# GpSimd reorders, ScalarE casts: swapping two steps of the q/k preparation between engines in an attention-plus-MLP kernel

## The chip, the core and the metric

The kernel runs on one core of one Trainium2 chip, as one program. The metric is the device time of one execution in microseconds. The engines named below are PE (TensorE, matrix multiply), ACT (ScalarE), DVE (VectorE), POOL (GpSimd) and SP (the queue that issues the DMAs). Each engine works through its own queue of instructions strictly in order.

## The reference

Local attention, attention over tokens pooled by four, and an MLP without bias (arrays are float32; B=8, H=8, S=576, D=64):

```python
q_d = q.reshape(B, H, Sd, 4, D).mean(axis=3)      # k_d, v_d alike, Sd = 144
out_d = softmax(scale * q_d @ k_d.T) @ v_d
out_up = np.repeat(out_d, 4, axis=2)
mask = np.abs(pos[:, None] - pos[None, :]) < 4    # a band of 7
out_local = softmax(where(mask, scale * q @ k.T, -1e9)) @ v
x = (out_up + out_local) as [B*S, H*D]            # 4608 x 512
h = x @ w_in                                      # 512 -> 2048
out = (h - tanh(h)) @ w_out                       # 2048 -> 512
```

## The kernel before

The attention is cut into 32 pairs, each two heads of one batch entry; four pairs make one batch entry. Pairs 0 to 7 and pairs 8 to 31 are prepared in two ways. From pair 8 (`EARLY`) on, a pair goes through these steps:

1. SP loads the rows of q and k as float32 into `qkn` (lines 325 to 340), nine tokens of 64 values on each of 64 partitions for each head; v goes to `vst`, and from pair 16 on a second copy of v to `vp`.
2. Two casts (line 490) write bfloat16 copies into `qr`, 128 x 576 each.
3. SP issues a DMA transpose, `qT<-qr` (line 495). Its result holds nine planes of 128 columns.
4. Two copies (line 503) put the planes in token order: `qk<-qT`, one for q and one for k. The input is read with a step of 128 bfloat16 values, the output written without a gap.
5. POOL adds tokens in fours: `half` (line 537) and `qkd` (line 543 or 550).
6. PE multiplies: scores of the band (line 559) and of the pooled part (line 582), in PSUM. ACT takes exponentials (lines 606, 618, 621). The band's mask is either multiplied into the exponentials `E` afterwards (the large one, 128 x 912, at line 610; the small one, 128 x 240, at line 625), or, from pair `FORE` on, the large one is added as a `bias` in PSUM before the exponential (line 601, DVE).
7. PE multiplies with v (lines 634, 640), DVE normalises (653, 655), a DMA transpose `lT<-ln` or PE turns the result, and a join (684, 688, on POOL or DVE) writes `xT`, the input of the MLP.

POOL also casts v (`vw`, line 424) and, from pair 16 on, pools v in two additions (`vp` 386, `vd` 391).

The MLP is `mm1` (line 727, then tanh on ACT at 738 and the subtraction on DVE at 741) and `mm2` (line 763, evacuated at 778 by ACT or DVE into `y`). Its matmuls use four PSUM banks, `ps_hy`.

The order on every engine is fixed when the program is built. The class `Program` holds each step with a cost in ns, its reads and writes and a priority; a list scheduler plays the plan through with these costs and appends the instructions in the order of the planned starts. An attention step of PE goes ahead of MLP matmuls as soon as the plan holds it ready; MLP matmuls fill the rest. A `P.choice` names several engines with a cost each, and the plan takes the one that comes free first. So a cost in the source changes the order of all queues, and where the cost is not the real one, a queue waits at run time.

In the kernel before, the casts of pairs 8 to 15 may run on DVE, ACT or POOL and those from pair 16 (`CASTS`) on POOL; the copies into token order run on ACT, and before pair 12 (`REORD`) also on DVE; `FORE` is 16.

Of the kernel before, what the change touches and what calls it, by code (L numbers as in the profile page):

```python
# [15 lines left out]
class Program:  # L16
# [20 lines left out]
    def op(self, eng, ns, fn, reads=(), writes=(), pri=0):  # L37
        i = len(self.ops)
        deps = set()
        for key in reads:  # L40
            if key in self.last_write:
                deps.add(self.last_write[key])
        for key in writes:
            if key in self.last_write:
                deps.add(self.last_write[key])
            deps.update(self.readers.get(key, ()))
        for key in reads:
            self.readers.setdefault(key, set()).add(i)
        for key in writes:
            self.last_write[key] = i  # L50
            self.readers[key] = set()
        deps.discard(i)
        if eng == "DMA":
            self.moves[i - 1] = i
        self.ops.append((eng, ns, fn, deps, pri))
        self.touch.append(set(reads) | set(writes))
        return i
# [108 lines left out]
def kernel(  # L166
# [83 lines left out]
    P = Program()  # L250
    op = P.op
    V, A, T, GP = nc.vector, nc.scalar, nc.tensor, nc.gpsimd
# [202 lines left out]
    def attention(p):  # L455
# [15 lines left out]
        if LOAD[p] == 'tok':  # L471
            P.choice([(eng, ns, lambda fn=fn: fn(
                out=qr[s].rearrange("p a h d -> p (a h d)"),
                in_=qkn[sn].rearrange("p h c -> p (h c)"))) for eng, ns, fn in CAST_QK],
                     reads=[("qkn", sn, 0), ("qkn", sn, 1)],
                     writes=[("qr", s, 0), ("qr", s, 1)], pri=pri - 12)
            if TIN[p] == 'dma':
                op("SP", 1300, lambda: nc.sync.dma_start_transpose(
                    out=qk[s].rearrange("p i c -> p (i c)").rearrange(
                        "p (t c) -> p t c", c=128),  # L480
                    in_=qr[s].rearrange("p a h d -> p (a h d)")),
                   reads=[("qr", s, 0), ("qr", s, 1)],
                   writes=[("qk", s, 0), ("qk", s, 1), ("qTq", s)], pri=-50)
                op("DMA", 1300, None, reads=[("qTq", s), ("qr", s, 0), ("qr", s, 1)],
                   writes=[("qk", s, 0), ("qk", s, 1)], pri=pri)
        else:
            for hh in range(2):
                dst = qr[s][:, :, hh]
                srt = qkn[sn][:, hh].rearrange("p (a d) -> p a d", d=D)
                P.choice([(eng, ns, lambda dst=dst, srt=srt, fn=fn: fn(out=dst, in_=srt))  # L490
                          for eng, ns, fn in (any3[2:] if p >= CASTS else any3[:1] + any3[2:] if 0 < p < NOACT else any3)],
                         reads=[("qkn", sn, 0), ("qkn", sn, 1)],
                         writes=[("qr", s, hh)], pri=pri - 12)
        if TIN[p] == 'dma' and LOAD[p] == 'row':
            op("SP", 1300, lambda: nc.sync.dma_start_transpose(
                out=qT[s], in_=qr[s].rearrange("p a h d -> p (a h d)")),
               reads=[("qr", s, 0), ("qr", s, 1)],
               writes=[("qT", s), ("qTq", s)], pri=-50)
            op("DMA", T_IN, None, reads=[("qTq", s), ("qr", s, 0), ("qr", s, 1)],
               writes=[("qT", s)], pri=pri)  # L500
            for i in range(2):
                def put(fn, i=i):
                    fn(out=full[:, i].rearrange("p (g a) -> p g a", a=A9),  # L503
                       in_=qT[s][:, :, i::2].rearrange("p a g -> p g a"))
                P.choice([("ACT", 1080, lambda put=put: put(A.copy))] +
                         [("DVE", 750, lambda put=put: put(V.tensor_copy))][:p < REORD],
                         reads=[("qT", s)], writes=[("qk", s, i)], pri=pri)
        elif TIN[p] == 'pe':
            if p in APART:
                parts = [(ps[:, 0].bitcast(BF16), 0, 5, ts, [("qk", s, 0)]),  # L510
                         (po[:, 0].bitcast(BF16), 5, 4, ox, [("qk", s, 1)])]
            else:
                parts = [(ps.rearrange("p b x -> p (b x)").bitcast(BF16), 0, A9, ts,
                          [("qk", s, 0), ("qk", s, 1)])]
            for bank, a0, n, keys, to in parts:
                planes = bank[:, 0:128 * n].rearrange("p (a x) -> p a x", a=n)

                def tr(planes=planes, a0=a0, n=n):
                    for a in range(n):
                        T.transpose(planes[:, a], qr[s][:, a0 + a].rearrange(  # L520
                            "p h d -> p (h d)"), ident)

                def put(fn, planes=planes, a0=a0, n=n):
                    fn(out=full.rearrange("p i (g a) -> p i g a", a=A9)[:, :, :, a0:a0 + n],
                       in_=planes.rearrange("p a (g i) -> p i g a", i=2))
                if a0 == 0:
                    P.fresh.add(len(P.ops))
                op("PE", (56 * n + 40) * cold, tr, reads=[("qr", s, 0), ("qr", s, 1), "ident"],
                   writes=keys, pri=pri)
                P.choice([("ACT", 90 + 98 * n, lambda put=put: put(A.copy)),  # L530
                          ("DVE", 60 + 140 * n, lambda put=put: put(V.tensor_copy))][:2 - (p in PUT_ACT)],
                         reads=keys, writes=to, pri=pri)
# [67 lines left out]
        def add_bias(bank, part):  # L600
            V.tensor_tensor(out=bank, in0=bank, op=ALU.add, in1=bias[:, part].unsqueeze(1)  # L601
                            .to_broadcast([128, 2, part.stop - part.start]))
        if p >= FORE:
            op("DVE", 1025, lambda: add_bias(ps[:, :, 0:456], slice(0, 456)),
# [3 lines left out]
           reads=ts, writes=[("E", s, 0)], pri=pri)  # L608
        if BIASED <= p < FORE:
            P.choice([(eng, ns, lambda fn=fn: fn(  # L610
                out=e1, in0=e1, in1=mask[:, 0:456].unsqueeze(1).to_broadcast([128, 2, 456]),
                op=ALU.mult)) for eng, ns, fn in MASK1[p >= NP]],
# [11 lines left out]
        if not biased:  # L624
            P.choice([(eng, ns, lambda fn=fn: fn(  # L625
                out=e2v, in0=e2v, in1=mask[:, 456:576].unsqueeze(1).to_broadcast([128, 2, 120]),
                op=ALU.mult)) for eng, ns, fn in MASK2[p >= SMALL][p >= FORE:]],
                reads=["mask"], writes=[("E", s, 1)], pri=pri)
# [16 lines left out]
        if p == 2:  # L645
# [13 lines left out]
            op=ALU.mult), reads=ox + [("r", s)], writes=[("ln", s)], pri=pri)  # L659
# [127 lines left out]
    def dense(kb):  # L787
# [6 lines left out]
        for _, second, i in steps:  # L794
# [6 lines left out]
    EARLY, BIASED = 8, 4  # L801
# [12 lines left out]
    INORDER = 6  # L814
    JOIN_V = [p for p in range(8, 32) if p % 4 > 1]
    V_ACT = ()
    FORE = 16
    GATE, BEHIND = range(12, NPAIR), 5
    BYACT = 0
    DIRECT, T_P = 16, 860  # L820
    T_IN, T_OUT = 1550, 1200
    NOACT = 0
    SMALL = 8
    HOLD = 3
    APART = (0, 1)
    LEAD = 0.75
    YOUT = [("ACT", 480, A.copy), ("DVE", 600, V.tensor_copy)]
    CASTS, REORD = 16, 12
    MASK1 = [[("DVE", 760, V.tensor_tensor)]] * 2
    MASK2 = [[("DVE", 300, V.tensor_tensor)], [("DVE", 300, V.tensor_tensor), ("POOL", 630, GP.tensor_tensor)]]  # L830
    T_Q0 = (850, 660), (2170, 1350), (710, 720), (700, 720)
# [6 lines left out]
    any3 = [("DVE", 670, V.tensor_copy), ("ACT", 590, A.copy),  # L838
            ("POOL", 630, GP.tensor_copy)]
# [53 lines left out]
    for p in range(2):  # L893
        prep_v(p)
    work = [attention(p) for p in range(NPAIR)]
    for a in work:
        next(a)
# [61 lines left out]
```

## Time and profile before

| | |
|---|---|
| median of 3 runs | 325.64 us (325.17 to 326.78) |
| the profiled execution | 325.69 us |
| its span, first to last instruction | 323.7 us |
| PE busy | 313.6 us, 97% of the span |
| DVE, ACT busy | 218.9 and 218.7 us, 68% each |
| POOL busy | 190.2 us, 59%, nothing after 250 us |
| granted TensorE clock | 1.00 throughout |

The profiled execution is 2.0 us longer than its span. A row of the profile names the line, the engine, the operation, output<-input by tile, shape and count, then the busy time in us, the mean of one in ns, and the idle time of the engine just ahead of these instructions with what ended it.

### The profile page before, as it was taken

The page shows a single profiled execution, that of the slowest core. Times are in us where ns is not written, and L with a number is a line of the kernel's source. Part 1 is how long each engine was busy: PE and PEld are TensorE (multiplying, and loading weights), DVE is VectorE, ACT ScalarE, POOL GpSimd, SP SyncE. Part 2 cuts the span into 40 slices and gives each one's busy share as a digit, 9 for nine tenths or more (in the row PEclk, how much of TensorE's full clock was granted, in tenths as well). Part 3 has the DMA queues.
Part 4 walks back from the last instruction along what each step waited for, and adds up shares of the span by engine and source line. Part 5 has one row for each costly group of instructions (what it writes and reads, how often), then busy time and mean ns, then how long its engine had stood idle before and what let it go on. Part 6 is the DMA issues. An engine that isn't in the chain of part 4 may idle for free.

```text
span 323.7 us, 7166 instructions
## 1 busy us (share of the span) xinstructions
PE 313.6 (97%) x2648; PEld 174.3 (54%) x2648; DVE 218.9 (68%) x395; ACT 218.7 (68%) x381; POOL 190.2 (59%) x262
## 2 busy tenths in 40 slices
PE   6898999999899999999999999999999999999996
PEld 2464555556654445666654444666654445566544
DVE  7898785678966589787785777777765554554311
ACT  3755886699877976898768877888786334545300
POOL 5658966278656897988887988889844000000000
PEclk9999999999999999999999999999999999999999
DMA  6999999989999899999999999999522211001022
GB/s 198 300 396 334 368 306 343 216 208 233 242 232 202 210 254 225 242 256 251 251 230 284 242 257 212 250 241 284 121 63 61 63 46 52 34 32 34 33 84 79
DMA packets 114515, 64.50 MB, mean 199 GB/s; under 512 B 92848, under 2 KB 97712, under 8 KB 114480
## 3 DMA queue, kind: packets, MB, share of 16 engines
q1 hardware_dynamic: 114480, 64.05, 79.9%
q8 instruction: 20, 0.33, 0.5%
q14 instruction: 15, 0.12, 0.1%
HBM read 42.47 MB, written 9.44 MB: 160 GB/s over the span
## 4 chain that ended last, share of the span: by engine, by line
PE 86%; SPq 5%; DMA 3%; DVE 2%; POOL 1%; issue 1%; ACT 1%; POOLq 0%; ACTq 0%
PE ps_hy L763 38%; PE ps_hy L727 36%; DMA gT<-in_moe_w_in_dram 3%; PE ps_ox L559 3%; PE ps_ox L634 3%; SPq L325 2%; SPq L358 2%; PE ps_ox L640 2%; PE ps_ox L582 1%; PE ps_ox L669 1%; DVE ln L655 1%; PE ps_ox L666 1%; PE ps_ox L520 1%; POOL w_in_sb L417 1%; DVE E L610 1%
## 5 line engine op out<-in xcount | busy, mean ns | idle before, releaser
L727 PE MATMUL ps_hy<-xT,w_in_sb 128*128 128x320 bf16 (+1 forms) x768 | 148.2, 326 | 1.1 <-DVE gT L741 1.1
L763 PE MATMUL ps_hy<-w_out_sb,gT 128*128 128x512 bf16 (+1 forms) x592 | 144.9, 373 | 0.0
L741 DVE TENSOR_TENSOR gT<-ps_hy,u 128x320 bf16<-128x320 f32 (+1 forms) x192 | 103.2, 553 | 61.0 <-ACT u L738 59.0
L738 ACT ACTIVATE u<-ps_hy 128x320 f32<-128x320 f32 (+1 forms) x192 | 92.2, 495 | 49.5 <-PE ps_hy L727 42.6
L727 PEld LDWEIGHTS <-w_in_sb 128*128 128x128 bf16 x768 | 71.8, 98 | 53.9 <-issue 1.5
L763 PEld LDWEIGHTS <-gT 128*128 128x128 bf16 x592 | 56.2, 98 | 53.3
L503 ACT COPY qk<-qT 128x576 bf16<-128x576 bf16 x44 | 52.4, 1208 | 0.0
L537 POOL TENSOR_TENSOR half<-qk 128x576 f32<-128x576 bf16 x29 | 33.3, 1147 | 27.5 <-ACT qk L503 18.9
L490 POOL CAST qr<-qkn 128x576 bf16<-128x576 f32 x51 | 34.4, 690 | 8.1 <-DMA qkn<-in_k_dram 4.6
L655 DVE TENSOR_TENSOR ln<-ps_ox,r 128x896 bf16<-128x896 f32 x32 | 34.9, 1091 | 1.0
L606 ACT ACTIVATE E<-ps_ox 128x912 bf16<-128x912 f32 x28 | 26.1, 932 | 5.0 <-PE ps_ox L559 4.0
L424 POOL CAST vw<-vst 128x640 bf16<-128x640 f32 x32 | 25.0, 781 | 3.8 <-DMA vst<-in_v_dram 3.5
L778 DVE COPY y<-ps_hy 128x512 f32<-128x512 f32 (+1 forms) x20 | 13.3, 663 | 16.7 <-PE ps_hy L763 16.5
L386 POOL TENSOR_TENSOR vp<-vp 72x512 f32<-72x512 f32 x16 | 20.3, 1270 | 1.0 <-DMA vp<-in_v_dram 1.0
L625 POOL TENSOR_TENSOR E<-E,mask 128x240 bf16<-128x240 bf16 x20 | 12.8, 641 | 11.6 <-ACT E L618 10.2
L634 PE MATMUL ps_ox<-vw,E 128*128 128x65 bf16 x320 | 19.6, 194 | 0.0
L634 PEld LDWEIGHTS <-E 128*128 128x128 bf16 x320 | 16.2, 98 | 5.6 <-DVE E L610 0.3
L621 ACT ACTIVATE E<-ps_ox 72x576 bf16<-72x576 f32 (+1 forms) x28 | 18.8, 671 | 0.0
L601 DVE TENSOR_TENSOR ps_ox<-ps_ox,bias 128x912 f32<-128x912 f32 x16 | 17.7, 1109 | 1.5 <-PE ps_ox L559 1.4
L640 PE MATMUL ps_ox<-vd,E 128*128 128x65 bf16 (+1 forms) x256 | 18.3, 193 | 0.1
L559 PEld LDWEIGHTS <-qk 64*128 64x128 bf16 x320 | 9.1, 94 | 15.5 <-issue 11.3
L778 ACT COPY y<-ps_hy 128x512 f32<-128x512 f32 x17 | 10.0, 587 | 7.1 <-PE ps_hy L763 7.1
(83 smaller groups left out, 266.6 us busy)
## 6 DMA issues: line engine op xcount, KB each, us to landing
vst<-in_v_dram SPq DMA_DIRECT2D x64, 160.0 KB, 4.2
qkn<-in_q_dram SPq DMA_DIRECT2D x32, 288.0 KB, 4.3
qkn<-in_k_dram SPq DMA_DIRECT2D x32, 288.0 KB, 4.3
out_dram<-y SPq DMA_DIRECT2D x35, 256.0 KB, 2.5
vp<-in_v_dram SPq DMA_DIRECT2D x16, 288.0 KB
gT<-in_moe_w_in_dram SPq DMA_DIRECT2D x4, 1024.0 KB, 11.0
xT<-in_moe_w_out_dram SPq DMA_DIRECT2D x8, 256.0 KB, 5.1
gT<-in_moe_w_out_dram SPq DMA_DIRECT2D x2, 1024.0 KB, 8.5
```

The costliest lines, as they stand in the source:

```text
L424: P.choice([(eng, ns, lambda fn=fn: fn(out=vw[w][:, 2 * jj:2 * jj + 2, :, 0:64], in_=vst[s])) for eng, ns, fn in CAST_V[p >= NEARLY]], rea ...
L490: P.choice([(eng, ns, lambda dst=dst, srt=srt, fn=fn: fn(out=dst, in_=srt)) for eng, ns, fn in (any3[2:] if p >= CASTS else any3[:1] + any ...
L503: fn(out=full[:, i].rearrange("p (g a) -> p g a", a=A9), in_=qT[s][:, :, i::2].rearrange("p a g -> p g a"))
L537: eng.tensor_tensor(out=half, in0=four[:, :, :, 0:2], in1=four[:, :, :, 2:4], op=ALU.add)
L606: op("ACT", 820, lambda: A.activation(out=e1, in_=ps[:, :, 0:456], func=AF.Exp, scale=SCALE), reads=ts, writes=[("E", s, 0)], pri=pri)
L634: T.matmul(po[:, hh, 65 * t:65 * t + 65], E[s][:, c:c + 128], vw[w][:, 2 * jj + hh, t, :], start=True, stop=True)
L640: T.matmul(po[:, hh, o:o + 65], E[s][0:kp, c + gw * i:c + gw * i + 128], vd[w][0:kp, jj, 2 * hh + i, :] if direct else vd[w][:, i, 2 * jj ...
L655: op("DVE", 1010, lambda: V.tensor_tensor(out=ln[s].rearrange("p n (h d) -> p h n d", d=D), in0=blocks[:, :, :, 0:64], in1=r[s].unsqueeze( ...
L727: T.matmul(ps_hy[slot][:, 0:n], w_in_sb[:, dc, fc * 128:(fc + 1) * 128], xT[dc][:, t0 + c0:t0 + c0 + n], start=(dc == 0), stop=(dc == N_DC ...
L738: op("ACT", 90 + 76 * n // 100, lambda: A.activation(out=u[us][:, 0:n], in_=ps_hy[slot][:, 0:n], func=AF.Tanh), reads=[("hy", slot)], writ ...
L741: op("DVE", 70 + 105 * n // 100, lambda: V.tensor_tensor(out=gT[g][:, fc, c0:c0 + n], in0=ps_hy[slot][:, 0:n], in1=u[us][:, 0:n], op=ALU.s ...
L763: T.matmul(ps_hy[slot][:, 0:c1 - c0], gT[g][:, fc, ts * 128:ts * 128 + 128], w_out_sb[:, fc, c0:c1], start=(fc == 0), stop=(fc == N_FF - 1))
```

## The change

Three parts, and tuning names that are no longer used go away:

- From pair 8 on both casts (step 2) run on ACT alone. Pairs 0 to 7 choose among three engines as before (`NOACT` was 0).
- From pair 8 on both copies into token order (step 4) run on POOL alone, planned at 650 ns.
- `FORE` goes from 16 to 12: pairs 12 to 15 get their large mask as an addition in PSUM before the exponential, and their small mask is multiplied by POOL alone.

```diff
@@ -488,7 +488,7 @@
                 P.choice([(eng, ns, lambda dst=dst, srt=srt, fn=fn: fn(out=dst, in_=srt))
-                          for eng, ns, fn in (any3[2:] if p >= CASTS else any3[:1] + any3[2:] if 0 < p < NOACT else any3)],
+                          for eng, ns, fn in any3[p >= EARLY:2 if p >= EARLY else 3]],
                          reads=[("qkn", sn, 0), ("qkn", sn, 1)],
                          writes=[("qr", s, hh)], pri=pri - 12)
@@ -502,8 +502,7 @@
                 def put(fn, i=i):
                     fn(out=full[:, i].rearrange("p (g a) -> p g a", a=A9),
                        in_=qT[s][:, :, i::2].rearrange("p a g -> p g a"))
-                P.choice([("ACT", 1080, lambda put=put: put(A.copy))] +
-                         [("DVE", 750, lambda put=put: put(V.tensor_copy))][:p < REORD],
+                op("POOL", 650, lambda put=put: put(GP.tensor_copy),
                          reads=[("qT", s)], writes=[("qk", s, i)], pri=pri)
@@ -814,18 +813,16 @@
-    FORE = 16
+    FORE = 12
...
-    NOACT = 0
...
-    CASTS, REORD = 16, 12
```

`any3` lists DVE at 670 ns, ACT at 590 and POOL at 630.

## The prediction

> **What bounds the kernel now.** I read the page first, then the stretches of 20 us, then PE's waits, then POOL's groups in the later attention stages. The page's engines, slices (PE and POOL) and chain:
>
> ```profile
> span 323.7 us, 7166 instructions
> PE 313.6 (97%) x2648; PEld 174.3 (54%) x2648; DVE 218.9 (68%) x395; ACT 218.7 (68%) x381; POOL 190.2 (59%) x262
> ...
> PE   6898999999899999999999999999999999999996
> ...
> POOL 5658966278656897988887988889844000000000
> ...
> PE 86%; SPq 5%; DMA 3%; DVE 2%; POOL 1%; issue 1%; ACT 1%; POOLq 0%; ACTq 0%
> ```
>
> PE is busy almost without a break from the fourth slice to the end. Attention, where POOL works, is over at about 250 us; the rest is MLP. Four of the stretches (time, then PE, PEld, DVE, ACT and POOL busy, clock, DMA share, GB/s), and PE's own waits:
>
> ```profile
> 60.00:80.00 20.00, 19.57 (x195) 11.74 (x194) 15.58 (x30) 17.64 (x35) 13.07 (x17) 1.00 1.05 226
> 80.00:100.00 20.00, 19.09 (x172) 10.98 (x171) 16.00 (x33) 17.28 (x33) 12.02 (x16) 1.00 1.13 239
> 100.00:120.00 20.00, 20.00 (x177) 9.89 (x176) 13.95 (x22) 16.11 (x23) 18.15 (x23) 1.00 0.99 218
> 220.00:240.00 20.00, 20.00 (x199) 12.44 (x197) 14.93 (x28) 16.37 (x30) 16.51 (x23) 1.00 0.64 156
> ```
>
> ```profile
> PE ps_hy L727 <- DVE gT L741: 1.1, 3, 0.6
> PE ps_ox L666 <- DVE ln L655: 0.4, 1, 0.4
> ```
>
> From 60 to 100 us PE misses 0.43 + 0.91 = 1.3 us, after that nothing until the end. The two built programs have the same PE order up to about 55 us, and the change leaves PE's work as it is. So what it can win is at most those 1.3 us and a few tenths in waits for DVE: PE is the bound, and no other engine's relief is worth more. What it can lose is not bounded in this way: PE's queue stands in a fixed order, and an attention matmul whose input is late holds up all MLP matmuls behind it.
>
> **The change part by part.** The rows that price it, both engines' casts and copies first:
>
> ```profile
> L503 ACT COPY qk<-qT 128x576 bf16<-128x576 bf16 x44 | 52.4, 1208 | 0.0
> L490 POOL CAST qr<-qkn 128x576 bf16<-128x576 f32 x51 | 34.4, 690 | 8.1 <-DMA qkn<-in_k_dram 4.6 <-DVE r L653 2.3 <-PE ps_ox L443 0.7
> L610 DVE TENSOR_TENSOR E<-E,mask 128x912 bf16<-128x912 bf16 x12 | 11.0, 919 | 3.2 <-ACT E L606 3.2
> L601 DVE TENSOR_TENSOR ps_ox<-ps_ox,bias 128x912 f32<-128x912 f32 x16 | 17.7, 1109 | 1.5 <-PE ps_ox L559 1.4
> L490 DVE CAST qr<-qkn 128x576 bf16<-128x576 f32 x7 | 5.2, 744 | 0.0
> L490 ACT CAST qr<-qkn 128x576 bf16<-128x576 f32 x6 | 4.0, 672 | 5.9 <-DMA qkn<-in_k_dram 5.9
> L503 DVE COPY qk<-qT 128x576 bf16<-128x576 bf16 x4 | 2.8, 709 | 0.0
> ```
>
> *Casts to ACT.* By the two built orders ACT goes from 6 to 52 casts and loses all 44 copies: 46 x 0.672 - 44 x 1.208 = -22 us of 218.7. POOL goes from 51 casts to 9, which takes away 42 x 0.690 = 29 us. A cast now waits on ACT for its load, and behind it stand exponentials and tanhs, hence `ps_hy` banks, hence PE. POOL's waits for that load were 4.6 us over the whole run; the later stages have 0.7 of it (below). I cost this at nothing, because the four banks hold MLP work behind a late tanh; if that cover is gone, it is the 0.7 us. On SP the transposes wait for the casts, and the next pair's loads stand behind them:
>
> ```profile
> L495 SPq DMA_TRANSPOSE qT<-qr x24: 1275/2040/2912, 56.4 to 231.6; - x24
> ```
>
> Their number and place hardly move and ACT is freer than POOL was, so nothing here either; a late one would add at most its own 2.9 us to one pair.
>
> *Mask of pairs 12 to 15.* Four multiplications at 0.919 after the exponential become four additions at 1.109 ahead of it: 0.19 us more on each of four pairs' way from score to output, up to 0.8 us, hidden by the MLP matmuls between a pair's scores and its output matmuls. One small mask moves from DVE to POOL.
>
> *Copies to POOL: the term that decides.* No row shows POOL reading `qT` with its step. From below: DVE did this copy in 709 against 744 for the cast, a factor 0.95, so 690 x 0.95 = 657 ns. From above: ACT did it in 1208 against 672, a factor 1.80, so 1240 ns. On the cast ACT and POOL are alike (672 and 690) and DVE is not, so I take the nearest row, ACT's own 1208. POOL then gains 48 x 1.208 - 29 = +29 us on 190, all of it before 250 us. The question is what POOL has to spare where attention is densest. From the end of `qkd` of pair 16 to that of pair 31, its stretch and its groups:
>
> ```profile
> 122.30:245.50 123.20, 123.20 (x1090) 70.77 (x1089) 91.50 (x155) 97.92 (x167) 102.20 (x135) 1.00 0.98 222
> ```
>
> ```profile
> L386 POOL TENSOR_TENSOR vp<-vp 72x512 f32<-72x512 f32 x14 | 17.8, 1271 | 1.0 <-DMA vp<-in_v_dram 1.0
> L490 POOL CAST qr<-qkn 128x576 bf16<-128x576 f32 x27 | 17.4, 667 | 0.7 <-DMA qkn<-in_k_dram 0.7
> L537 POOL TENSOR_TENSOR half<-qk 128x576 f32<-128x576 bf16 x15 | 17.2, 1146 | 10.8 <-ACT qk L503 10.7
> L391 POOL TENSOR_TENSOR vd<-vp 72x256 bf16<-72x256 f32 x14 | 10.5, 748 | 0.7
> L543 POOL TENSOR_TENSOR qkd<-half 128x288 bf16<-128x288 f32 x15 | 10.3, 683 | 0.2
> L424 POOL CAST vw<-vst 128x640 bf16<-128x640 f32 x14 | 10.1, 722 | 2.3 <-DMA vst<-in_v_dram 2.3
> L625 POOL TENSOR_TENSOR E<-E,mask 128x240 bf16<-128x240 bf16 x15 | 9.6, 641 | 5.4 <-ACT E L618 5.3
> L688 POOL TENSOR_TENSOR xT<-lT 128x336 bf16<-128x336 bf16 x10 | 7.7, 767 | 0.0
> L684 POOL TENSOR_TENSOR xT<-lT 128x240 bf16<-128x240 bf16 x11 | 6.6, 599 | 0.0
> ```
>
> POOL is busy 102.2 of 123.2 us. Of its 21 us of idle time, 10.7 are the wait for ACT's copies, which goes away since POOL now makes them; 5.3 wait for exponentials and 4.0 for loads. The groups add up to 107.2 us, 5.0 more than the engine was busy, over 135 instructions: neighbours overlap by 37 ns, which I take off each.
>
> The tightest part of the new order is from the `qkd` of pair 17 to that of pair 29. It holds 12 vp, 13 vd, 13 vw, 12 half, 12 qkd, 13 masks and 9 joins of two instructions: 93 instructions, 76.9 us by the rows' means, 73.5 after the overlap. To these come 24 copies: 24 x (1.208 - 0.037) = 28.1. POOL needs 101.6 us. What PE gives it is the time between the scores of the same pairs, and the lead that POOL has at the start. From the order of time, PE's score groups of pairs 17 and 29 and POOL's `qkd` of pair 17:
>
> ```profile
> 136.49 0.42 PE L559 MATMUL ps_ox<-qk 64*128 64x120 bf16 x10
> ```
>
> ```profile
> 231.03 0.43 PE L559 MATMUL ps_ox<-qk 64*128 64x120 bf16 x10
> ```
>
> ```profile
> 129.10 0.93 POOL L543 TENSOR_TENSOR qkd<-half 128x288 bf16<-128x288 f32 x1
> ```
>
> Before, that is 231.0 - 136.5 = 94.5 us, and POOL led by 136.5 - 130.0 = 6.5 us. In the new order fewer MLP matmuls stand in between: 240 of 512 columns instead of 246, and 192 of 320 columns instead of 202. The chain gives their price, 0.215 and 0.136 us each:
>
> ```profile
> 298.83 1.09 PE ps_hy L727 x8
> 299.92 0.86 PE ps_hy L763 x4
> ```
>
> That is 2.7 us less, so 91.8 us, plus the lead of 6.5: 98.3. POOL is short by 101.6 - 98.3 = 3.3 us without a single wait. Waits for exponentials and loads were 9.3 us in the longer stretch; a POOL that comes late finds most of them over, and I keep 3 (bounds 0 and 8). PE then stands still for 3.3 + 3 = 6.3 us in all, which nothing behind it can take back, since PE is the bound until the end. **The sum:** 325.69 + 6.3 - 0.3 (what the relieved ACT may give of the 1.3 us) = 331.7 us. The profiled run lies 0.05 us from the median, so this stands as it is.
>
> The Trainium skill, in "GPSIMD Engine Reference", section "Performance pitfalls for Q7 kernels", says that reading SBUF with a step of over 8 bytes costs about half as much again for each element, and here the step is 256 bytes; it speaks against the change. By it, an estimate, a copy takes 1.5 x 0.690 = 1.035 us, POOL comes 0.8 us inside its limit without waits, and with 3 us of waits the kernel loses 2 us: 327.5. No run here shows that price yet.
>
> **The rivals.**
>
> *POOL copies at the price of a cast* (657 to 800 ns). At 657 the tight part takes 73.5 + 24 x 0.62 = 88.4 us, under 91.8 even without a lead. Then PE never waits; the time stays within 1 us, 324.8 to 326.5. For it: DVE reads the same pattern without loss. Against it: ACT pays 80%. The border with the forecast is (98.3 - 73.5 - 3) / 24 + 0.037 = 0.95 us for a copy.
>
> *Faster: ACT's relief reaches PE.* PE's one stretch with gaps, 60 to 100 us, is also where ACT is fullest (17.6 and 17.3 of 20 us). With ACT 22 us lighter the tanhs come sooner, the waits for gT go, and the score of each early pair stands earlier. It wins the 1.3 us and the 0.4 us of the wait for ln at the most: 324.0. It decides only if a copy on POOL costs under 0.8 us. Against it: this is the whole of what PE has to give.
>
> *ACT's casts hold up the tanhs.* A cast that waits for its load stands ahead of tanh and exponential. The wait that POOL had, 0.7 us in the later stages and up to 4.6 in all, moves to ACT with PE behind it; from that 1 to 3 us: 326.7 to 328.7. Against it: ACT has 25 us idle in the stretch above.
>
> **How the numbers follow.** Some 0.5% (1.6 us) is what a measurement of this kernel can tell from no change. The forecast, POOL short, has 0.60; of it nearly all is slower. POOL at the cast's price has 0.25, nearly all within 0.5%. The relief that reaches PE has 0.07, faster. ACT's casts 0.08, slower by the larger part. So faster 0.07, same 0.27, slower 0.66. The low end is the rival without any stall and with part of PE's gaps won: 324.5. The high end is the upper price, 1240 ns (0.8 us more than the forecast), all 8 us of waits and a lead of only 3 us instead of 6.5: 3.3 + 0.8 + 8 + 3.5 = 15.6, so 341.
>
> **What would show it.** In the changed kernel's profile: `qk<-qT` on POOL x48 with a mean near 1.2 us; POOL without idle from about 120 to 245 us, its wait for ACT's copies gone; PE under 20.00 in several 20 us stretches after 120 us, with PE or its weight loads waiting for POOL's qkd or E; attention ending near 250 us instead of ending sooner. If the copies show 0.7 us and PE stays full, the price was wrong and with it the forecast. If PE waits for ACT's u or for DVE's gT instead, the third rival holds. If the copies cost 1.2 us and PE is still full, the lead or the waits were wrong.

## The result, and the profile after

The changed kernel takes 341.61 us (median of 6 runs, 341.17 to 342.61) against 325.43 us before (median of 6): a ratio of 1.0493, 95% interval 1.046 to 1.0527. Slower was forecast, with 331.7 us; the time lies just over the range's upper end of 341.0. The profiled execution took 342.51 us. Runs over 1.5% above the fastest of their kernel are left out of every comparison, which matters once, for the kernel with the plan at 1200 ns below: its 334.3 and 335.3 us count, its 342.1 us, which was the profiled execution, and 342.8 us do not.

The page: engines, the slices of PE and POOL, the granted clock, and the chain.

```profile
span 340.8 us, 7133 instructions
PE 319.9 (94%) x2648; PEld 176.7 (52%) x2648; DVE 227.5 (67%) x379; ACT 203.2 (60%) x392; POOL 216.3 (63%) x267
...
PE   6999999999999991999989995999999999999996
...
POOL 5678654598969999189999998499994000000000
PEclk9999999999999998799999997899999999999999
...
PE 76%; POOL 9%; DVE 8%; DMA 3%; ACT 2%; issue 1%; SPq 0%; ACTq 0%; POOLq 0%
```

PE has one slice at 1 tenth and one at 5, and behind each of them the clock falls. POOL is at 9 in most slices from there to 250 us, and falls to 1 right behind the first hole and to 4 behind the second. The chain now goes through DVE for 8% of the span and through POOL for 9%, and PE's share falls from 86% to 76%. By stretches of 20 us, the two with the holes and one beside each:

```profile
100.00:120.00 20.00, 20.00 (x161) 9.54 (x160) 11.79 (x18) 13.71 (x25) 19.84 (x23) 1.00 1.18 231
120.00:140.00 20.00, 12.62 (x90) 6.42 (x89) 16.76 (x15) 8.41 (x16) 17.45 (x20) 0.83 0.74 177
...
200.00:220.00 20.00, 15.82 (x116) 7.46 (x114) 14.19 (x13) 9.11 (x16) 14.79 (x18) 0.83 0.78 195
220.00:240.00 20.00, 20.00 (x179) 12.36 (x174) 13.65 (x24) 15.22 (x33) 19.33 (x23) 1.00 1.04 223
```

PE stands still for 7.4 us in the first hole and 4.2 us in the second. Its own waits name the tile, and the groups give the prices:

```profile
PE ps_hy L726 <- DVE xT L687: 7.4, 1, 7.4
PE ps_ox L558 <- DVE ln L654: 4.2, 1, 4.2
PE ps_ox L633 <- POOL E L624: 2.1, 2, 1.5
```

```profile
L503 POOL COPY qk<-qT 128x576 bf16<-128x576 bf16 x48 | 56.3, 1202 | 7.7 <-DMA qT<-qr 7.7
L490 ACT CAST qr<-qkn 128x576 bf16<-128x576 f32 x52 | 33.8, 675 | 3.9 <-DMA qkn<-in_k_dram 3.9
L683 DVE TENSOR_TENSOR xT<-lT 128x240 bf16<-128x240 bf16 x7 | 15.2, 2166 | 0.0
L687 DVE TENSOR_TENSOR xT<-lT 128x336 bf16<-128x336 bf16 x7 | 9.6, 1367 | 0.0
```

The copies cost 1202 ns and the casts 675, as predicted (1208 and 672). But the two long waits of PE are for DVE, not for POOL. DVE's joins, each two additions with both inputs in SBUF, took 2166 and 1367 ns on the average. The order of time shows what that average is made of. DVE, POOL and PE around the first hole (start, duration, instruction):

```profile
126.20 6.61 DVE L683 TENSOR_TENSOR xT<-lT 128x240 bf16<-128x240 bf16 x1
132.73 3.20 DVE L687 TENSOR_TENSOR xT<-lT 128x336 bf16<-128x336 bf16 x1
135.86 0.68 DVE L740 TENSOR_TENSOR gT<-ps_hy,u 128x512 bf16<-128x512 f32 x1
```

```profile
125.70 0.73 POOL L424 CAST vw<-vst 128x640 bf16<-128x640 f32 x1
126.39 1.15 POOL L536 TENSOR_TENSOR half<-qk 128x576 f32<-128x576 bf16 x1
...
130.60 0.73 POOL L424 CAST vw<-vst 128x640 bf16<-128x640 f32 x1
131.27 1.27 POOL L386 TENSOR_TENSOR vp<-vp 72x512 f32<-72x512 f32 x1
132.62 0.77 POOL L391 TENSOR_TENSOR vd<-vp 72x256 bf16<-72x256 f32 x1
133.34 2.23 POOL L503 COPY qk<-qT 128x576 bf16<-128x576 bf16 x2
135.65 1.29 POOL L536 TENSOR_TENSOR half<-qk 128x576 f32<-128x576 bf16 x1
```

```profile
121.10 1.03 PE L762 MATMUL ps_hy<-w_out_sb,gT 128*128 128x512 bf16 x4
...
128.18 0.43 PE L726 MATMUL ps_hy<-xT,w_in_sb 128*128 128x320 bf16 x2
135.99 2.89 PE L726 MATMUL ps_hy<-xT,w_in_sb 128*128 128x320 bf16 x10 [7.38 <-DVE xT L687]
138.68 1.64 PE L762 MATMUL ps_hy<-w_out_sb,gT 128*128 128x512 bf16 x4
```

The first half of a join, which takes 0.4 us undisturbed, stays in DVE for 6.6 us. Its transposed input had landed at 123.8, before it began. From 125.70 on POOL's instructions follow one another without a break; the first is at 131.27 + 1.27 = 132.54, where `vd` waits 0.08 us for what `vp` has written. The first half ends at 132.81, 0.27 us behind the start of that break. The second half then lasts through POOL's `vd` and two copies, up to the next break (133.34 + 2.23 = 135.57), and ends at 135.93. All the while the MLP's matmuls wait for `xT`. When PE goes on, four matmuls of 512 columns take 1.64 us where they took 1.03 before the hole, and the stretch from 136 to 140 us (PE, PEld, DVE, ACT, POOL busy, clock) shows why:

```profile
136.00:140.00 4.00, 4.00 (x14) 1.93 (x14) 2.95 (x6) 2.58 (x5) 1.61 (x2) 0.51 0.00 0
```

The granted clock is 0.51. Of the 17.1 us that the span grew by, 10.8 are idle time of PE (20.9 instead of 10.1) and 6.3 are longer busy time. Most of that is the clock, by an estimate: 4.0 us at 0.51 here and 6.2 us at 0.54 behind the second hole (209.3 to 215.5 us) lose 4.0 x 0.49 + 6.2 x 0.46 = 4.8 us.

In the second hole PE waits for a normalisation, `ln`, that stands behind a join in DVE's queue:

```profile
201.22 5.34 DVE L683 TENSOR_TENSOR xT<-lT 128x240 bf16<-128x240 bf16 x1
208.12 1.09 DVE L654 TENSOR_TENSOR ln<-ps_ox,r 128x896 bf16<-128x896 f32 x1
```

### The profile page after: what moved, and what is told of

Read it like the earlier page. It is cut to its first block, busy times and chain, and to the rows that moved or that the text cites. A ratio compares the mean times of both kernels' runs of the same rounds, so it can differ in the third digit from the quotient of the medians.

```text
span 340.8 us, 7133 instructions
## 1 busy us (share of the span) xinstructions
PE 319.9 (94%) x2648; PEld 176.7 (52%) x2648; DVE 227.5 (67%) x379; ACT 203.2 (60%) x392; POOL 216.3 (63%) x267
## 4 chain that ended last, share of the span: by engine, by line
PE 76%; POOL 9%; DVE 8%; DMA 3%; ACT 2%; issue 1%; SPq 0%; ACTq 0%; POOLq 0%
PE ps_hy L726 32%; PE ps_hy L762 31%; DVE xT L683 3%; POOL qk L503 3%; PE ps_ox L558 3%; PE ps_ox L633 2%; PE ps_ox L639 2%; DMA vp<-in_v_dram 2%; POOL vp L386 1%; POOL half L536 1%; DVE xT L687 1%; POOL E L624 1%; PE ps_ox L668 1%; DMA qkn<-in_k_dram 1%; DVE ln L654 1%
## 5 line engine op out<-in xcount | busy, mean ns | idle before, releaser
L503 POOL COPY qk<-qT 128x576 bf16<-128x576 bf16 x48 | 56.3, 1202 | 7.7 <-DMA qT<-qr 7.7
L490 ACT CAST qr<-qkn 128x576 bf16<-128x576 f32 x52 | 33.8, 675 | 3.9 <-DMA qkn<-in_k_dram 3.9
L624 POOL TENSOR_TENSOR E<-E,mask 128x240 bf16<-128x240 bf16 x21 | 14.1, 670 | 20.0 <-ACT E L617 20.0
L600 DVE TENSOR_TENSOR ps_ox<-ps_ox,bias 128x912 f32<-128x912 f32 x20 | 22.3, 1114 | 6.2 <-PE ps_ox L558 6.2
L777 ACT COPY y<-ps_hy 128x512 f32<-128x512 f32 x26 | 15.3, 588 | 8.5 <-PE ps_hy L762 8.4
L617 ACT ACTIVATE E<-ps_ox 128x240 bf16<-128x240 f32 x28 | 10.5, 374 | 14.2 <-PE ps_ox L581 9.0
## 6 DMA issues: line engine op xcount, KB each, us to landing
gT<-in_moe_w_in_dram SPq DMA_DIRECT2D x4, 1024.0 KB, 10.8
```

Source lines behind the costliest of these rows:

```text
L503: fn(out=full[:, i].rearrange("p (g a) -> p g a", a=A9), in_=qT[s][:, :, i::2].rearrange("p a g -> p g a"))
```

## The experiments

Theory A: DVE gets the second tile of a join only where POOL stops, and a POOL without breaks holds up DVE and through it PE. Theory B: POOL is short of time, as predicted, and the joins only suffer with it.

**All joins on POOL.**

```diff
-    JOIN_V = [p for p in range(8, 32) if p % 4 > 1]
+    JOIN_V = []
```

> The changed kernel with all joins on POOL (JOIN_V empty), so that DVE has no operation on lT left. Theory A (POOL without a break keeps DVE's joins, which read two tiles in SBUF, waiting; DVE then holds up PE): the two long stalls of PE (7.4 and 4.2 us, with the half clock behind them) are gone although POOL has 7 joins more (7 x 1.38 = 9.7 us); what is left are short waits of PE for POOL: 326 to 333 us. Theory B (POOL is short of time, as predicted, and the joins on DVE only suffer with it): POOL is 9.7 us shorter still, so 345 to 352 us.

331.85 us, ratio 1.0207 (1.0169 to 1.0245). PE's waits, and a stretch:

```profile
PE ps_ox L633 <- POOL E L624: 2.9, 7, 0.9
PE ps_hy L726 <- POOL xT L687: 2.2, 3, 0.9
```

```profile
180.00:200.00 20.00, 19.48 (x159) 9.78 (x158) 11.59 (x16) 13.23 (x24) 19.92 (x26) 1.00 1.05 257
```

POOL makes seven joins more and is busy 223.4 us in all instead of 216.3, 19.92 of 20 us in this stretch, and the kernel is 9.8 us faster than the changed one. No wait of PE is over 0.9 us in this part of the run. Theory B's 345 to 352 us do not come. But the plan was made anew for this run, so the orders of the queues moved with the joins; the next two experiments leave them alone.

**Breaks put into POOL's queue.**

```diff
+            if p >= 14:
+                GP.tensor_copy(out=junk[:, 1:2], in_=vw[w][:, 2 * jj, 0, 0:1])   # behind the v cast
...
+                    GP.tensor_copy(out=junk[:, 0:1], in_=qkd[s][:, 0, 0:1])      # behind qkd, pair >= 16
```

> The changed kernel with more work on POOL: behind each v cast from pair 14 on, and behind each qkd from pair 16 on, POOL copies one element of what it has just written. Each of these 34 small copies waits for POOL's own last write, so POOL stands still for a moment on both sides of it. The plan and all orders else are the same. Theory A (DVE's joins get their second tile in SBUF only when POOL stops between two instructions): each join starts at the next such break, the longest join of DVE falls from 6.6 us to under 3.5 us, PE's stalls of 7.4 and 4.2 us shrink with it, and the time falls by 5 to 11 us to 331 to 337 although POOL has some 8 us more to do. Theory B (POOL is short of time): 345 to 350 us.

336.04 us, ratio 1.0328 (1.0313 to 1.0343): 5.6 us less than the changed kernel, with more work on the engine that is full. The joins on DVE by their lines (minimum, median and maximum in ns):

```profile
L688 DVE TENSOR_TENSOR xT<-lT x7: 398/576/1997, 91.7 to 266.0; 128x240 bf16<-128x240 bf16 x7
L692 DVE TENSOR_TENSOR xT<-lT x7: 496/1023/1477, 92.0 to 266.3; 128x336 bf16<-128x336 bf16 x7
PE ps_ox L638 <- POOL E L629: 8.7, 11, 2.0
```

The longest first half of a join falls from 6606 to 1997 ns and both holes are gone. PE's instructions and POOL's, but for the small copies, come in the same order as in the changed kernel. Theory B falls: it gave 345 to 350. What is left is PE waiting for POOL, which is now really short.

**The joins taken off DVE without loading POOL.** Two plain copies on ACT in place of the addition; the pooled part is left out for seven pairs.

```diff
+                A.copy(out=x0..., in_=lT[s][:, 0:5:4, 0:120])
+                A.copy(out=x[:, 120:456]..., in_=lT[s][:, 1:4, 0:112])
-            P.choice([("DVE", 1500, lambda: join(V))][:p in JOIN_V] +
+            P.choice([("DVE", 1500, copy_only)][:p in JOIN_V] +
```

> The changed kernel with the seven joins of DVE given to ACT, which has room, and cut down there to two plain copies of lT into xT: the pooled part is left out for these pairs. POOL's queue and load are those of the changed kernel, and DVE has no join. Theory A splits the 16 us: what the joins cost goes away, what POOL's shortage costs stays: 327 to 332 us, with PE waiting for POOL's E and for little else. If the joins on DVE were only a symptom, the time stays at 338 to 342 us.

327.05 us, ratio 1.0045 (1.0016 to 1.0074). A stretch, and PE's main wait in the attention stages:

```profile
200.00:220.00 20.00, 20.00 (x185) 12.26 (x184) 14.19 (x25) 14.72 (x31) 20.00 (x25) 1.00 1.06 258
```

```profile
PE ps_ox L633 <- POOL E L624: 1.8, 4, 0.7
```

In this stretch POOL is busy 20.00 of 20 us, and PE is too. PE's and POOL's instructions come in the same order as in the changed kernel, so only the joins and what they release have changed. This splits the 16.2 us: POOL's shortage costs about 1.5 (0.5 to 2.4 by the interval), the joins on DVE about 14.6.

**FORE.** Back to 16, first in the changed kernel, then without joins on DVE.

```diff
-    FORE = 12
+    FORE = 16
```

> The changed kernel with FORE back at 16: pairs 12 to 15 multiply the large mask into E on DVE, from two tiles in SBUF, as in the kernel before. The prediction cost this part at nothing: 340 to 343 us. Under theory A the four multiplications are four more operations of DVE that wait for a break of POOL: they take over 1.5 us each, and the time is 342 to 347 us.

> The same with FORE at 16, as in the kernel before. With the joins on DVE, FORE 16 was 7.5 us faster than FORE 12 (334.1 against 341.6). If FORE acts only through the place where DVE's join of pair 14 meets POOL's queue, then without these joins the two differ by less than 2 us: 326 to 333 us. If the addition in PSUM costs time by itself, FORE 16 stays 5 us or more ahead of the run with FORE 12.

With the joins on DVE 334.08 us, ratio 1.0265 (1.0247 to 1.0284), 7.5 us less than the changed kernel; neither number that was expected holds. Of the four multiplications two took 1.61 and 1.63 us and two 0.63 and 0.77, where theory A had all four over 1.5. Without them 327.61 us, ratio 1.0064 (1.0032 to 1.0096), against 327.05. So FORE costs nothing by itself that these runs can tell. The join of pair 14 with FORE at 16:

```profile
126.23 2.60 DVE L683 TENSOR_TENSOR xT<-lT 128x240 bf16<-128x240 bf16 x1
128.75 1.45 DVE L687 TENSOR_TENSOR xT<-lT 128x336 bf16<-128x336 bf16 x1
```

It begins at the same time as with FORE at 12 (126.20), but POOL's queue stands in another order there:

```profile
126.26 2.30 POOL L503 COPY qk<-qT 128x576 bf16<-128x576 bf16 x2
128.65 1.19 POOL L536 TENSOR_TENSOR half<-qk 128x576 f32<-128x576 bf16 x1
```

`half` waits for the two copies, so POOL has a break at 126.26 + 2.30 = 128.56, 2.3 us after the join began, and the first half of the join ends 0.27 us behind it. The first hole is gone with that; the second one, 4.2 us, stays.

**The price of the copy.** The same change with a plain copy on POOL, the reordering left out; and with the reordering done on the side of the write.

```diff
-                    fn(out=full[:, i].rearrange("p (g a) -> p g a", a=A9),
-                       in_=qT[s][:, :, i::2].rearrange("p a g -> p g a"))
+                    fn(out=full[:, i].rearrange("p (a g) -> p a g", a=A9), in_=qT[s][:, :, i::2])  # plain
+                    fn(out=full[:, i].rearrange("p (g a) -> p a g", a=A9), in_=qT[s][:, :, i::2])  # other way round
```

> The changed kernel with the copies on POOL reading and writing without a gap: the reordering into token order is left out, all else is the same, the planned cost too. A copy should take 650 to 700 ns instead of 1202. Both theories: POOL has its breaks again, DVE's joins stay under 1.6 us, PE is full from 55 us on: 324.5 to 327 us, which is what the prediction's rival 'POOL copies at the price of a cast' gave (324.8 to 326.5). If it stays over 330 us, something else in the change costs time: the casts on ACT or the earlier addition of the mask.

> The changed kernel with the copies into token order written the other way round: they read qT in its own order (steps of 4 bytes) and write with a step of 18 bytes. Same values, same planned cost. If the price of a copy on POOL comes from the read, it falls from 1202 ns to 650 to 750 ns, POOL gets its breaks back, and under both theories PE is full again: 324 to 327 us. If the price comes from the strided side whichever it is, the copy stays near 1200 ns and the time near 341.6 us.

> The kernel before with the copies into token order (ACT, and DVE before pair 12) written the other way round: they read qT in steps of 4 bytes and write with a step of 18. Same values. On POOL this order took 2875 instead of 1202 ns. If ACT's price of 1208 comes from its read of 256-byte steps, a copy falls to 670 to 750 ns, ACT loses about 22 us, and PE, which is the bound, gains at most 1.3 us: 324 to 325.5 us. If ACT pays for strided writes as POOL does, 1300 to 2900 ns and 328 us or more.

The plain copy writes without a gap, but it still reads every second column, a step of 4 bytes. It took 325.39 us, ratio 1.0 (0.9984 to 1.0016). Its group and DVE's join:

```profile
L503 POOL COPY qk<-qT 128x576 bf16<-128x576 bf16 x48 | 30.8, 669 | 9.2 <-DMA qT<-qr 4.8 <-PE ps_hy L726 4.4
L683 DVE TENSOR_TENSOR xT<-lT 128x240 bf16<-128x240 bf16 x7 | 6.1, 866 | 0.3 <-DMA lT<-ln 0.3
```

The longest first half of a join was 2.10 us, where under 1.6 was expected; in the attention stages PE waited 0.5 us at most for DVE. So the rest of the change, casts on ACT and FORE, neither costs nor wins more than 0.2% once POOL's copy is cheap. The other way round was expected to be cheap and is not: 397.23 us with POOL, ratio 1.2223 (1.218 to 1.2266), and 373.16 us in the kernel before, ratio 1.1452 (1.1385 to 1.1519). The copy's group, with POOL and then in the kernel before on ACT and DVE:

```profile
L503 POOL COPY qk<-qT 128x576 bf16<-128x576 bf16 x48 | 128.2, 2875 | 4.7 <-DMA qT<-qr 4.7
```

```profile
L503 ACT COPY qk<-qT 128x576 bf16<-128x576 bf16 x44 | 120.1, 2810 | 0.0
L503 DVE COPY qk<-qT 128x576 bf16<-128x576 bf16 x4 | 10.9, 2718 | 0.0
```

**The plan told the real price.**

```diff
-                op("POOL", 650, lambda put=put: put(GP.tensor_copy),
+                op("POOL", 1200, lambda put=put: put(GP.tensor_copy),
```

> The changed kernel with the planned cost of a copy on POOL at 1200 instead of 650, which is what it takes; only orders and choices move. Theory A: the plan spreads attention, but POOL is planned nearly full and so stays without breaks, and more joins go to DVE; stalls stay, 330 to 342 us. Theory C (the loss comes from the wrong cost in the plan alone): 325 to 328 us.

334.8 us, ratio 1.0294 (1.0245 to 1.0344). Theory C falls: a plan with the real price still loses. In the profiled execution the first half of a join is longer still, and again ends 0.27 us after an instruction of POOL (136.41 + 1.25 = 137.66):

```profile
128.79 9.14 DVE L683 TENSOR_TENSOR xT<-lT 128x240 bf16<-128x240 bf16 x1
```

```profile
136.41 1.25 POOL L386 TENSOR_TENSOR vp<-vp 72x512 f32<-72x512 f32 x1
```

**The casts alone on ACT**, the copies left there.

```diff
-   for eng, ns, fn in (any3[2:] if p >= CASTS else any3[:1] + any3[2:] if 0 < p < NOACT else any3)],
+   for eng, ns, fn in (any3[1:2] if p >= EARLY else any3)],
```

> The kernel before with one part of the change alone: from pair 8 on the casts run on ACT; copies into token order stay on ACT (DVE too before pair 12), FORE stays 16. POOL loses about 29 us, ACT gains about 31 us (near 250 of 324 us busy). Theory A and B: POOL has breaks everywhere, DVE's joins take 0.4 to 0.8 us, PE stays full: 324.5 to 327 us. Rival: ACT becomes the engine that comes late, tanhs stand behind casts and copies, and PE waits for banks: 328 to 335 us.

333.23 us, ratio 1.0251 (1.0212 to 1.0291). The engines, and what POOL waits for:

```profile
PE 316.6 (96%) x2648; PEld 175.4 (53%) x2648; DVE 211.0 (64%) x383; ACT 243.2 (73%) x431; POOL 165.4 (50%) x224
```

```profile
POOL half L537 <- ACT qk L503: 41.7, 19, 6.5
```

The time lies in the rival's range, and ACT is the engine that comes late: POOL waits 41.7 us for its copies, where it was 18.9 before. But the rival's path is not what PE's waits show. They name ACT's exponential once, for 2.0 us, and DVE's join once, for 1.7 us; those for `gT`, which stands behind the tanh, are 1.1 us in all, as before. How the 8.2 us (333.23 against 325.06 for the kernel before in the same series) come about stays open. A join's first half took up to 1.21 us there, where 0.4 to 0.8 was expected.

## Why the prediction was right or wrong

- *PE is the bound and has 1.3 us to give.* Right. The stretches from 60 to 100 us are full in the changed kernel, and with a plain copy the time is the old one.
- *A copy on POOL takes 1208 ns.* Right: 1202. Half as much again, which the Trainium skill states ("GPSIMD Engine Reference", "Performance pitfalls for Q7 kernels"), is too little here: 669 ns with a step of 4 bytes and 1202 with 256 is a factor of 1.80. ACT's factor, from cast to copy, was 1.80 too; why the two engines pay alike and DVE does not, no run shows.
- *POOL is busy without idle time from about 120 us on.* Right in part: POOL is busy in both holes, but behind them it waits for exponentials itself, 8.2 us from 137.6 us on and 4.6 us from 216.1 on.
- *POOL is short by 3.3 us, and 3 us of waits stay.* Mis-sized. With POOL's queue unchanged and no join on DVE the loss was about 1.5 us, and PE waited 1.8 us for POOL's E. POOL had 0.0 to 0.2 us of idle time in most stretches there: the 3 us of waits that were kept went to nothing, and part of the 3.3 with them.
- *The step that failed:* the cost of the full POOL was looked for on POOL's own way to PE alone. DVE's joins kept the price that they had while POOL had breaks. That missing term is worth about 14.6 us with its half-clock tail, against 6.3 for the one that was priced. So slower was forecast for a cost that made about 1.5 of the 16.2 us, and that the range ends near the measured time is luck: its upper end was made of POOL's waits and lead. The profile of before had the sign, in the spread of two rows (minimum, median and maximum in ns):

```profile
L610 DVE TENSOR_TENSOR E<-E,mask x12: 623/760/2143, 32.7 to 121.2; 128x912 bf16<-128x912 bf16 x12
L601 DVE TENSOR_TENSOR ps_ox<-ps_ox,bias x16: 1100/1106/1117, 130.0 to 248.0; 128x912 f32<-128x912 f32 x16
```

  The large mask multiplication on DVE, with two tiles in SBUF, took up to 2143 ns; the addition in PSUM kept to 1117 wherever it stood.
- *FORE costs nothing.* Right by itself (327.05 and 327.61 us), wrong in this kernel: it moved the order in which pair 14's join met POOL, and 7.5 us went with it.
- *The rivals.* POOL at a cast's price gave 324.8 to 326.5; the plain copy measured 325.39. Casts on ACT that hold up the rest did not decide here, with ACT at 203.2 us; where ACT kept the copies it came late. None named DVE as the engine that comes late.

What stays open: why a join gets in at one end of a POOL instruction and is passed over at the next. That DVE gets in *only* at breaks, as theory A has it, is too strong. In the changed kernel the first halves that lasted 6.6 and 5.3 us ended at the first break after their start, but the second half of another join got in where POOL went straight on, one instruction after it began:

```profile
177.50 1.45 DVE L687 TENSOR_TENSOR xT<-lT 128x336 bf16<-128x336 bf16 x1
177.40 1.19 POOL L536 TENSOR_TENSOR half<-qk 128x576 f32<-128x576 bf16 x1
178.55 0.90 POOL L624 TENSOR_TENSOR E<-E,mask 128x240 bf16<-128x240 bf16 x1
```

What the runs do show is that joins on DVE beside a full POOL last long and hold up PE, and that breaks put into POOL's queue, or joins taken off DVE, end that. The Trainium skill ("SBUF — State Buffer", "SBUF: two separate sides") says that DVE and GpSimd share a pair of ports, which one instruction holds to its end while the other waits. The ends fit that: in the changed kernel and with the plan at 1200 ns, every first half of a join that lasted over 2 us ended 0.27 us behind the end of a POOL instruction. The lengths do not: one instruction of POOL took 1.3 us at most there, and first halves of 9.1, 6.6 and 5.3 us were seen, over five or more instructions of POOL.

## What to carry to other kernels

When an engine is brought to full load, price not only its own queue but every other engine's operations that were quick because it had breaks; here GpSimd's full queue cost more through VectorE's additions of two SBUF tiles than through GpSimd's own lateness. Here it paid to give such additions to the full engine itself, although that added work to it (331.85 us instead of 341.61). And where a stall comes out of two fixed queues meeting, a change elsewhere that only moves the order can be worth as much as the change that one means to measure.

## What the runs showed of the hardware that was not expected

- An addition of 128x240 on DVE with both inputs in SBUF took 0.40 us with POOL idle (at 272 us, behind the attention), and with POOL running without a break 6.61 us in the changed kernel and 9.14 us with the plan at 1200 ns.
- Writing 128x576 bfloat16 values with a step of 18 bytes cost 2875, 2810 and 2718 ns on POOL, ACT and DVE; the read with a step of 256 bytes and a gapless write cost 1202, 1208 and 709.
- After PE had stood still for 7.4 us the granted clock was 0.51 in the next 4 us, so that stall cost more than its length.
